# A spectral mixing layer and two feed-forward layers on one core: where the sum of real and imaginary part is made

## The chip, the cores and the metric

The kernel runs on one core of one Trainium2 chip. The metric is the device time of one execution in microseconds (us): 1951.52 as the median of three runs, which lie between 1948.21 and 1952.62.

The engines of a core work side by side, each through its own list of instructions in a fixed order, and wait for each other by semaphores. TensorE (PE in the rows) multiplies matrices and writes to PSUM, the small memory for its results; it loads the weights of a product in instructions of their own (PEld). VectorE (DVE) and ScalarE (ACT) read PSUM and the main on-chip memory, SBUF. GpSimd (POOL) and SyncE (SP) here only start transfers.

## The reference

Three layers follow each other, on 4 batches of 3072 rows with 256 columns. The first mixes along the rows by a real Fourier transform, a complex product with a bias, a soft threshold, and the transform back:

```
X = rfft(x, axis=1)
Yr = Xr @ w_r - Xi @ w_i + b_r
Yi = Xr @ w_i + Xi @ w_r + b_i
Y  = sign(Y) * max(|Y| - 0.01, 0)        # real and imaginary part apart
y  = irfft(Y)
```

The second shifts by one row, mixes with two vectors, and computes `sigmoid(xr @ w_r) * (relu(xk @ w_k)**2 @ w_v)` (hidden width 1024). The third computes `g = h * clip(h + 3, 0, 6) / 6` with `h = x @ w_in`, and then `g @ w_out` (hidden width 2048). Everything is float32.

## The kernel before

**The transform.** The 3072 rows are 96 by 32. Stage `s1` multiplies by a 96-point table over all rows of a batch; its results go to DRAM and come back in another order. Function `mid(b)` then does the middle of the transform for one batch in 12 steps `j`. Each step has four parts. `s2(j)` multiplies the data (as weights) by a table `t` (as the moving side): four products, one for each half of the frequencies `g` and of the 256 columns `dt`. In batches 1 to 3 the table has 192 columns, three groups of 64: real part, imaginary part, and their sum. The sum is a third set of table columns, so TensorE computes it. `mix(j)` makes the complex product from three real ones (sum times w_r, imaginary part times -(w_r + w_i), real part times w_i - w_r), adds the bias and applies the threshold. `split_y(j)` and `ia(j)` begin the transform back; `ib` ends it after another trip through DRAM.

**Precision.** A float32 product of `s2` is carried out as two passes on TensorE. The products after it are float32r, in one pass, and get their precision from splitting each operand into a high part and a rest: `split` rounds with a ScalarE copy (line 167) and subtracts with VectorE (line 168). So the result of `s2`, a PSUM tile of 128 x 768 numbers, becomes the tiles `Xh` and `Xl`. In `mix` each pair of operands takes three products (function `three`, line 176).

**Order.** The engines' order is that in which the code is written. The batches' middle stage is a generator, `stream(later)`, of which `feed()` takes one step at a time between the units of the second layer: `u_r` (tile `pr`), `u_k` (tile `pk`; the ReLU of line 719, the square of lines 723 and 727, the rest of line 728) and `u_v` (tile `acc`). A round of the middle stage is thus, on TensorE, a `pk` or `pr`, an `ia`, an `s2` (tile `s` in the rows), an `acc` and a `mix`. On VectorE a round has the square and its rest (727, 728), the threshold of the mix before (453), the rest of `s2` (`Xl`, 168), that of `split_y` (`yl`, 168), and the two sums after the mix (`yf`, 448 and 449); now and then also steps of `prep`, which makes the input of the next tile of the second layer (682, 690). On ScalarE it has the first half of the threshold (`ym`, 451), parts of `prep` (677, 688), the square's high part (`gh`, 723), the ReLU (719), the copy of `ia` (488), `Xh` (167) and `yh` (167).

**PSUM.** The results of `pk`, `pr`, `s2`, `mix`, `ia`, `s1` and `ib` share three buffers that are taken in turn (`ptile`). A product into a buffer waits until the third one before it has been read. In the middle stage `s2` thus often takes the buffer of a `mix`, and waits for line 449, which reads it last. A `pk` or an `ia` takes that of an `s2`, and waits for `Xl`.

The lines that the change touches are in `_tables` (the order of the table's columns), `load_t` (which columns are loaded), `s2` and `part` of `mix`:

Of the kernel before, what the change touches and what calls it, by code (L numbers as in the profile page):

```python
# [9 lines left out]
F32 = mybir.dt.float32  # L10
# [3 lines left out]
AF = mybir.ActivationFunctionType  # L14
# [7 lines left out]
NP = NG // 2  # L22
# [4 lines left out]
BEHIND = 3  # L27
# [18 lines left out]
def _pair(a):  # L46
    hi = _round12(a)
    return hi, (a - hi.astype(np.float64)).astype(np.float32)


def _tables():

    th = 2 * np.pi / S
    n1 = np.arange(N1)
    n2 = np.arange(N2)
    f1 = np.zeros((N1, N1))
    f1[:, 0] = 1.0
    f1[:, 1] = (-1.0) ** n1
    for u in range(1, 48):
        f1[:, 2 * u] = np.cos(2 * np.pi * u * n1 / N1)  # L60
        f1[:, 2 * u + 1] = -np.sin(2 * np.pi * u * n1 / N1)
    fwd = np.zeros((NP, 2, 2, 2, N2, 4, N2))
    inv = np.zeros((NP, 2, 2, 2, N2, 2, 2, N2))
    for g in range(NG):
        for uu in range(2):
            u = 2 * g + uu
            m = np.zeros((2, N2, 2, N2))
            w = np.zeros((2, N2, 2, N2))
            if u:
                k = u + N1 * np.arange(N2)  # L70
                s = np.where(k <= S // 2, 1.0, -1.0)
                c, z = np.cos(th * np.outer(n2, k)), np.sin(th * np.outer(n2, k))
                m[0, :, 0], m[1, :, 0] = c, z
                m[0, :, 1], m[1, :, 1] = -z * s, c * s
                w[0, :, 0], w[1, :, 0] = c.T * 2 / S, (-z * s).T * 2 / S
                w[0, :, 1], w[1, :, 1] = z.T * 2 / S, (c * s).T * 2 / S
            else:
                for j in range(N2):
                    src = 0 if j < 16 else 1
                    f = N1 * j if j < 16 else N1 // 2 + N1 * (j - 16)  # L80
                    c, z = np.cos(th * f * n2), np.sin(th * f * n2)
                    if j == 0:
                        alt = (-1.0) ** n2
                        m[0, :, 0, 0], m[0, :, 1, 0] = 1.0, alt
                        w[0, 0, 0], w[1, 0, 0] = 1.0 / S, alt / S
                    else:
                        m[src, :, 0, j], m[src, :, 1, j] = c, -z
                        w[0, j, src], w[1, j, src] = c * 2 / S, -z * 2 / S
            m = np.concatenate([m, m.sum(2, keepdims=True), 0 * m[:, :, :1]], 2)
            if u == 0:  # L90
                m[0, :, 2, 0], m[0, :, 3, 0] = 1.0, alt - 1.0
                m[:, :, 0:2, 0] = 0.0
            fwd[g // 2, uu, g % 2] = m
            inv[g // 2, uu, :, g % 2, :, g % 2] = w
    ext = np.zeros((128, N2), np.float32)
    ext[0:64] = fwd[0, 0, 0, :, :, 3].reshape(64, N2)
    fwd = fwd[:, :, :, :, :, 0:3].transpose(0, 1, 3, 4, 2, 5, 6)
    wide = np.zeros((NP, 2, 2, N2, 2, 3, 2, N2))
    for uu in range(2):
        wide[:, uu, :, :, :, :, uu] = fwd[:, uu]  # L100
    tab = np.zeros((NP + BEHIND, 128, 2, 448), np.float32)
    tab[:NP, :, :, 0:192] = wide.reshape(NP, 128, 2, 192)
    by_part = inv.reshape(NP, 2, 128, 128).transpose(0, 2, 1, 3)
    tab[BEHIND :, :, :, 192:448] = np.concatenate(_pair(by_part), 3)
    tab0 = np.zeros((NP + BEHIND, 128, 2, 224), np.float32)
    tab0[:NP, :, :, 0:96] = fwd.reshape(NP, 128, 2, 96)
    by_half = inv.reshape(NP, 2, 2, 64, 128).transpose(0, 1, 3, 2, 4)
    place = np.arange(128).reshape(4, 8, 4).transpose(1, 0, 2).ravel()
    tab0[BEHIND :, :, :, 96:224] = by_half.reshape(NP, 128, 2, 128)[..., place]
    rows = np.arange(N1).reshape(NP, 2, 2, 2).transpose(0, 2, 1, 3).reshape(-1)  # L110
    small = np.concatenate([f1, f1.T[rows]], 1).astype(np.float32)
    return [np.ascontiguousarray(a) for a in (tab, tab0, ext, small)]
# [3 lines left out]
def fourier_mix_ffn_kernel(  # L116
# [20 lines left out]
    nc = tc.nc  # L137
# [19 lines left out]
    def pad(pool, n):  # L157

        pads.append(n)
        pool.tile([128, n // 4], F32, name=f"pad{len(pads)}")  # L160

    def ptile(name):
        return ps.tile([128, 1024], F32, tag="h", name=name)

    def split(src, h, l):

        nc.scalar.activation(h, src, AF.Copy)
        nc.vector.tensor_sub(l, src, h.bitcast(F32))
# [86 lines left out]
    with tc.manual_schedule(engines=order):  # L255
        ff = ctx.enter_context(ExitStack())
        fp = ff.enter_context(tc.tile_pool(name="fp", bufs=1, side="right"))
# [40 lines left out]
        def take(n):  # L298

            u = head["use"]  # L300
            load_chunks(u + n)
            r = [live.pop(u + i) for i in range(n)]
            head["use"] = u + n
            return r
# [52 lines left out]
        def load_t(b, j):  # L357

            if j >= NP + BEHIND:
                b, j = b + 1, j - NP - BEHIND  # L360
            if b < B:
                if pad_t:
                    pad(fp, pad_t.pop())
                t = fp.tile([128, 2, 448], F32R if b else F32, tag="t", bufs=3, name="tt")
                n, w = (192, 448) if b else (96, 224)
                c = slice(0 if j < NP else n, n if j < BEHIND else w)
                nc.gpsimd.dma_start(out=t[:, :, c], in_=(tab if b else tab0)[j, :, :, c])
                tt[b, j] = t

        def mid(b):  # L370
# [9 lines left out]
            def s2(j):  # L380
                (a,) = take(1)
                t = tt[b, j].bitcast(F32) if b else tt[b, j]
                p = ptile("s2")
                if pad_x:
                    pad(fp, pad_x.pop())
                xh = fp.tile([128, 896], F32R, tag="Xh", bufs=2, name="Xh")
                xl = fp.tile([128, 896], F32R, tag="Xl", bufs=2, name="Xl")
                mm = lambda o, lhs, rhs: nc.tensor.matmul(o, lhs, rhs, start=True, stop=True)  # L388
                for g in range(2):
                    for dt in range(2):  # L390
                        d = slice(128 * dt, 128 * dt + 128)
                        if b:
                            o = p[:, 512 * dt : 512 * dt + 384].rearrange("p (k h g f) -> p k h g f", k=3, h=2, g=2)
                            mm(o[:, :, :, g], a[:, g, d], t[:, g, 0:192])
                        else:
                            for h in range(2):
                                k = slice(64 * h, 64 * h + 64)
                                c = 512 * h + 192 * dt
                                o = p[:, c : c + 192].rearrange("p (k g f) -> p k g f", k=3, g=2)
                                mm(o[:, :, g], a[k, g, d], t[k, g, 0:96])  # L400
                        if not (j or g):
                            c = 384 + (512 if b else 32) * dt
                            k = slice(0, 128 if b else 64)
                            mm(p[:, c : c + 32], a[k, g, d], tex[k])
                if b:
                    v = p.rearrange("p (dt f) -> p dt f", dt=2)
                    w = lambda x: x[:, 0:768].rearrange("p (dt f) -> p dt f", dt=2)
                    split(v[:, :, 0:384], w(xh), w(xl))
                    e = v[:, :, 384:416]
                else:  # L410
                    v = p.rearrange("p (h f) -> p h f", h=2)[:, :, 0:384].rearrange("p h (c f) -> p h c f", f=64)
                    w = lambda x: x[:, 0:768].rearrange("p (c h f) -> p h c f", c=6, h=2)
                    split(v, w(xh), w(xl))
                    e = p[:, 384:448].rearrange("p (dt f) -> p dt f", dt=2)
                if not j:
                    w = lambda x: x[:, 768:832].rearrange("p (dt f) -> p dt f", dt=2)
                    split(e, w(xh), w(xl))
                xx[j] = (xh, xl)

            def mix(j):  # L420
                xh, xl = xx.pop(j)
                p = ptile("mix")
                k1 = p[:, 512:768]

                def part(k):
                    cs = [slice(384 * dt + 128 * k, 384 * dt + 128 * k + 128) for dt in range(2)]
                    if k == 3:
                        cs = [slice(768 + 32 * dt, 800 + 32 * dt) for dt in range(2)]
                    return [((xh[:, c], xl[:, c]), dt) for dt, c in enumerate(cs)]
# [807 lines left out]
```

## Time and profile before

| | us |
|---|---|
| median of three runs | 1951.52 |
| the profiled execution | 1950.81 |
| its span, first to last instruction | 1948.6 |
| PE busy | 1916.4 (98%) |
| DVE busy | 1419.5 (73%) |
| ACT busy | 1237.6 (64%) |
| mean granted clock of TensorE | 0.993 |

The middle stages of batches 1 to 3 lie between about 145 and 252, 336 and 452, and 527 and 642 us of the span. The rest of the time up to about 990 us belongs to the other stages of the transform and the second layer, and the time from there to the third layer. The profile's busy time of PE counts pipelined products with modelled ends; a gap between two of them is time in which TensorE waited.

### The profile page before, as it was taken

Reading aid. Unit: us, or ns where it says so; the run is one execution under the profiler, and the core shown is the slowest. Engines: PE = TensorE matmul, PEld = TensorE weight load, DVE = VectorE, ACT = ScalarE, POOL = GpSimd, SP = SyncE. Lnnn points to the kernel's source line nnn. Section 1 sums busy time; section 2 is a strip of 40 time slices with the busy share of each in tenths; the row PEclk is TensorE's granted clock in tenths of the full one; section 3 lists DMA queues with packets and bytes.
Section 4 is the critical chain, followed back from the end, with each engine's and each line's share of the span. In section 5 each row is a group of like instructions: output and inputs, shape, how many; then the busy total and the mean of one; then the engine's idle time right before and its main releaser. Section 6 shows DMA issues by size and latency. Waiting matters only on the chain.

```text
span 1948.6 us, 32994 instructions
## 1 busy us (share of the span) xinstructions
PE 1916.4 (98%) x13512; PEld 1756.6 (90%) x13512; DVE 1419.5 (73%) x1770; ACT 1237.6 (64%) x1770; POOL 136.5 (7%) x245
## 2 busy tenths in 40 slices
PE   8989999999999999999999999999999999999998
PEld 5778878887888788888899999999999999999998
DVE  3867655675566657787688777887778887788876
ACT  3665554556445457777567767676677766677765
POOL 2402320222022100000000000000000000000000
PEclk8989999999999999999999999999999999999999
DMA  8784567456634442221101001010010100011000
GB/s 274 220 265 139 155 179 237 118 145 198 223 103 122 135 152 77 84 91 67 44 23 34 23 23 33 23 33 23 23 28 28 33 23 23 24 33 34 23 12 23
DMA packets 106593, 172.80 MB, mean 89 GB/s; under 512 B 13827, under 2 KB 63795, under 8 KB 106443
## 3 DMA queue, kind: packets, MB, share of 16 engines
q1 hardware_dynamic: 88714, 132.87, 21.6%
q0 software_dynamic: 17296, 37.53, 7.3%
q8 instruction: 106, 1.74, 0.4%
q14 instruction: 45, 0.36, 0.1%
q10 hardware_dynamic: 432, 0.30, 0.1%
HBM read 97.71 MB, written 63.31 MB: 83 GB/s over the span
## 4 chain that ended last, share of the span: by engine, by line
PE 92%; DVE 4%; DMA 1%; ACT 1%; issue 1%; SPq 0%; POOL 0%; ACTq 0%; DVEq 0%; POOLq 0%
PE oacc L988 26%; PE rq L988 16%; PE acc L176 13%; PE pk L176 13%; PE cc L988 6%; PE mix L176 4%; PE pr L176 3%; PE s L388 3%; PE ib L575 3%; PE s L323 2%; PE ia L176 1%; PE pi L176 1%; DVE g L920 0%; DMA a<-sc_b 0%; ACT g L916 0%
## 5 line engine op out<-in xcount | busy, mean ns | idle before, releaser
L988 PE MATMUL oacc<-wo_hi,gl 128*128 128x256 f32 x1536 | 425.2, 277 | 1.2 <-DVE gl L929 1.2
L988 PE MATMUL oacc<-wo_hi,gh 128*128 128x256 f32 x1536 | 425.3, 277 | 0.0
L988 PE MATMUL oacc<-wo_lo,gh 128*128 128x256 f32 x1536 | 424.7, 276 | 0.0
L988 PEld LDWEIGHTS oacc<-wo_hi,gl 128*128 128x128 f32 x1536 | 288.7, 188 | 1.8 <-DVE gl L929 1.6
L988 PEld LDWEIGHTS oacc<-wo_hi,gh 128*128 128x128 f32 x1536 | 288.4, 188 | 0.2
L988 PEld LDWEIGHTS oacc<-wo_lo,gh 128*128 128x128 f32 x1536 | 288.5, 188 | 0.0
L920 DVE SCALAR_TENSOR_TENSOR g<-g,c 128x1024 f32<-128x1024 f32 x184 | 225.5, 1225 | 50.2 <-ACT g L916 47.5
L929 DVE TENSOR_TENSOR gl<-g,gh 128x1024 fp32r<-128x1024 f32 x184 | 225.2, 1224 | 41.2 <-ACT gh L926 41.2
L916 ACT ACTIVATE g<-c,half 128x1024 f32<-128x1024 f32 x184 | 212.2, 1153 | 4.9 <-DVE c L911 4.9
L988 PE MATMUL rq<-th,sw 128*128 128x256 f32 x1104 | 206.1, 276 | 0.0
L906 ACT ACTIVATE s<-rq 128x256 f32<-128x256 f32 x184 | 70.5, 383 | 209.6 <-PE rq L988 209.5
L926 ACT ACTIVATE gh<-g 128x1024 fp32r<-128x1024 f32 x184 | 193.8, 1053 | 1.7 <-DVE g L920 1.6
L910 DVE TENSOR_TENSOR c<-rq,s 128x512 f32<-128x512 f32 x184 | 126.6, 688 | 89.1 <-ACT s L906 89.0
L988 PEld LDWEIGHTS rq<-th,sw 128*128 128x128 f32 x1104 | 166.3, 188 | 0.2 <-ACT s L895 0.2
L176 PE MATMUL pk<-kh,wk_hi 128*128 128x512 f32 x384 | 156.3, 407 | 0.4 <-DVE yf L449 0.4
L176 PE MATMUL acc<-gh,wv_hi 128*128 128x512 f32 x384 | 155.0, 404 | 0.0
L988 PE MATMUL rq<-tl,sw 128*128 128x256 f32 x552 | 152.5, 276 | 0.7 <-DVE tl L864 0.7
L176 PE MATMUL acc<-gl,wv_hi 128*128 128x512 f32 x384 | 150.7, 392 | 0.5 <-DVE gl L728 0.5
L176 PE MATMUL acc<-gh,wv_lo 128*128 128x512 f32 x384 | 150.3, 391 | 0.0
L176 PE MATMUL pk<-kl,wk_hi 128*128 128x512 f32 x384 | 150.2, 391 | 0.0
L176 PE MATMUL pk<-kh,wk_lo 128*128 128x512 f32 x384 | 149.6, 390 | 0.0
L727 DVE TENSOR_TENSOR g<-g 128x1024 f32<-128x1024 f32 x76 | 92.9, 1222 | 77.5 <-ACT gh L723 77.0
(174 smaller groups left out, 4449.6 us busy)
## 6 DMA issues: line engine op xcount, KB each, us to landing
yt<-sc_y SPq DMA_DIRECT2D x23, 608.0 KB, 3.9
sc_a<-s1sb SPq DMA_DIRECT2D x32, 384.0 KB, 6.5
a<-sc_a SPq DMA_DIRECT2D x48, 256.0 KB, 3.3
sc_b<-iasb SPq DMA_DIRECT2D x48, 256.0 KB, 4.1
sc_y<-ysb SPq DMA_DIRECT2D x32, 384.0 KB, 2.6
sc_x<-r SPq DMA_DIRECT2D x24, 512.0 KB, 2.8
xa<-sc_x SPq DMA_DIRECT2D x24, 512.0 KB, 3.8
tt<-in_tab_dram POOLq DMA_DIRECT2D x27, 448.0 KB, 3.8
```

The source lines that it names most:

```text
L176: nc.tensor.matmul(o, a, c, start=first and i == 0, stop=last and i == n - 1, **kw)
L323: nc.tensor.matmul(p[:N1, 512 * i : 512 * i + 512], f1, a, start=True, stop=True)
L388: mm = lambda o, lhs, rhs: nc.tensor.matmul(o, lhs, rhs, start=True, stop=True)
L575: nc.tensor.matmul(p[:, q, et, i], lhs, fi, start=True, stop=True)
L727: nc.vector.tensor_mul(g, g, g)
L906: nc.scalar.activation(s[:, 3], q, AF.Copy)
L910: nc.vector.tensor_add(c[:, 1::2], two(rq), s[:, 0:2])
L916: nc.scalar.activation(g, c, AF.Relu, bias=half, scale=1.0 / 6.0)
L920: nc.vector.scalar_tensor_tensor(g, g, 1.0, tmp["c"], op0=ALU.min, op1=ALU.mult)
L926: nc.scalar.activation(h, tmp["g"], AF.Copy)
L929: nc.vector.tensor_sub(hg[i, j][1], tmp["g"], hg[i, j][0].bitcast(F32))
L988: return lambda: nc.tensor.matmul(o, lhs, rhs, start=start, stop=stop, skip_group_check=True)
```

## The change

For the steps `j` from 1 on in batches 1 to 3, `s2` multiplies only by the 128 table columns of the real and imaginary part, and the sum is made from the two results. The table's three groups are put in the order sum, real, imaginary; the load leaves the first group out. ScalarE copies the imaginary part (128 x 2 x 128) from PSUM to a new SBUF tile `im`; VectorE adds it to the real part and writes the sum into the free third of the PSUM tile; ScalarE makes the high part of real and imaginary in one instruction and that of the sum in a second; VectorE makes the rest in one, as before. Step 0 of each batch, with its special columns, and batch 0 stay as they were. `mix` finds its operands under the new order of the groups.

```diff
-        wide[:, uu, :, :, :, :, uu] = fwd[:, uu]
+        wide[:, uu, :, :, :, :, uu] = fwd[:, uu][..., (2, 0, 1), :]
...
-                c = slice(0 if j < NP else n, n if j < BEHIND else w)
+                c = slice((64 if b and j else 0) if j < NP else n, n if j < BEHIND else w)
...
-                            mm(o[:, :, :, g], a[:, g, d], t[:, g, 0:192])
+                            k = 1 if j else 0
+                            mm(o[:, k:, :, g], a[:, g, d], t[:, g, 64 * k : 192])
...
-                    split(v[:, :, 0:384], w(xh), w(xl))
+                    if j:
+                        s = fp.tile([128, 2, 128], F32, tag="im", bufs=1, name="im")
+                        nc.scalar.activation(s, v[:, :, 256:384], AF.Copy)
+                        nc.vector.tensor_add(v[:, :, 0:128], v[:, :, 128:256], s)
+                        nc.scalar.activation(w(xh)[:, :, 128:384], v[:, :, 128:384], AF.Copy)
+                        nc.scalar.activation(w(xh)[:, :, 0:128], v[:, :, 0:128], AF.Copy)
+                        nc.vector.tensor_sub(w(xl), v[:, :, 0:384], w(xh).bitcast(F32))
+                    else:
+                        split(v[:, :, 0:384], w(xh), w(xl))
...
                 def part(k):
+                    if b and k < 3:
+                        k = (k + 1) % 3
```

The engines' order follows the code. On ScalarE, around step 4 of batch 3 (the tile `s` is the PSUM tile of `s2`, `iasb` the copy of `ia`; the semaphores that a row waits for stand in brackets), these are the rows of before:

```order
L719 ACTIVATE g<-pk 128x1024 [waits PE_49]
L488 ACTIVATE iasb<-ia 128x512 [waits PE_49]
L167 ACTIVATE Xh<-s_4982 128x768 [waits PE_49]
L167 ACTIVATE yh<-yz 128x512 [waits DMASW2_49,DMASW3_49,DMASW1_49,DMASW0_49]
L688 ACTIVATE kh<-xf 128x1024 [waits DVE_49]
L723 ACTIVATE gh<-g 128x1024 [waits Activation_49]
```

and these the rows of the changed kernel at the same place, with its own line numbers:

```order
L730 ACTIVATE g<-pk 128x1024 [waits PE_49]
L499 ACTIVATE iasb<-ia 128x512 [waits PE_49]
L411 ACTIVATE im<-s_5082 128x256 [waits PE_49]
L413 ACTIVATE Xh<-s_5082 128x2x256 [waits DVE_49]
L414 ACTIVATE Xh<-s_5082 128x2x128
L167 ACTIVATE yh<-yz 128x512 [waits DMASW2_49,DMASW3_49,DMASW1_49,DMASW0_49]
L699 ACTIVATE kh<-xf 128x1024
L734 ACTIVATE gh<-g 128x1024 [waits Activation_49]
```

One instruction has become three, and the second of them waits for VectorE; `yh`, `kh` and `gh` stand behind it.

On VectorE at the same place, before:

```order
L727 TENSOR_TENSOR g<-g 128x1024 [waits Activation_49]
L728 TENSOR_TENSOR gl<-g,gh 128x1024 [waits DVE_49]
L682 SCALAR_TENSOR_TENSOR xf<-yt,mus,xf 128x512 x2
L453 SCALAR_TENSOR_TENSOR yf<-ym,yf 128x512
L168 TENSOR_TENSOR Xl<-s_4982,Xh 128x768 [waits Activation_49]
L168 TENSOR_TENSOR yl<-yz,yh 128x512 [waits DMASW2_49,DMASW1_49,DMASW3_49,DMASW0_49,Activation_49]
L727 TENSOR_TENSOR g<-g 128x1024 [waits Activation_49]
```

and after:

```order
L738 TENSOR_TENSOR g<-g 128x1024 [waits Activation_49]
L739 TENSOR_TENSOR gl<-g,gh 128x1024 [waits DVE_49]
L693 SCALAR_TENSOR_TENSOR xf<-yt,mus,xf 128x512 x2
L464 SCALAR_TENSOR_TENSOR yf<-ym,yf 128x512
L412 TENSOR_TENSOR s_5082<-s_5082,im 128x2x128 [waits Activation_49]
L415 TENSOR_TENSOR Xl<-s_5082,Xh 128x768 [waits Activation_49]
L168 TENSOR_TENSOR yl<-yz,yh 128x512 [waits DMASW2_49,DMASW1_49,DMASW3_49,DMASW0_49,Activation_49]
L738 TENSOR_TENSOR g<-g 128x1024 [waits Activation_49]
```

The sum has been put in between the threshold of the mix before and `Xl`; nothing else has moved.

## Rows read from the trace of the kernel before

**Rows 1.** Busy time by stretch: us, each engine with (instructions), clock, DMA share, GB/s.

```profile
120.00:226.00 106.00, 106.00 (x606) 93.38 (x604) 77.97 (x97) 60.19 (x81) 19.14 (x36) 1.00 0.55 168
```

**Rows 2.** Timeline of TensorE: start, us, engine, line, operation, tiles, shape, merged count, [idle before].

```profile
559.64 1.46 PE L388 MATMUL s<-tt,a 128*128 128x192 f32 x8
...
96.56 2.00 PE L575 MATMUL ib<-fi,rows 96*128 96x96 f32 x16 [0.21 <-DMA stw<-in_moe_w_v_dram]
```

**Rows 3.** Timeline of TensorE, the three passes of s2 before which it waited.

```profile
227.51 1.54 PE L388 MATMUL s<-tt,a 128*128 128x192 f32 x8 [1.36 <-issue]
...
398.56 1.54 PE L388 MATMUL s<-tt,a 128*128 128x192 f32 x8 [1.38 <-issue]
...
571.48 1.62 PE L388 MATMUL s<-tt,a 128*128 128x192 f32 x8 [2.06 <-issue]
```

**Rows 4.** Timeline of VectorE ahead of the third of these waits, batch 3.

```profile
547.50 0.69 DVE L448 TENSOR_TENSOR yf<-mix,bias 128x512 f32<-128x512 f32 x1 [1.70 <-PE mix L176]
...
554.66 0.95 DVE L168 TENSOR_TENSOR Xl<-s,Xh 128x768 fp32r<-128x768 f32 x1
...
557.98 0.69 DVE L449 TENSOR_TENSOR yf<-yf,mix 128x512 f32<-128x512 f32 x1
561.69 1.22 DVE L727 TENSOR_TENSOR g<-g 128x1024 f32<-128x1024 f32 x1 [3.02 <-ACT gh L723]
...
566.02 0.95 DVE L168 TENSOR_TENSOR Xl<-s,Xh 128x768 fp32r<-128x768 f32 x1
...
567.58 1.23 DVE L727 TENSOR_TENSOR g<-g 128x1024 f32<-128x1024 f32 x1
...
570.70 0.69 DVE L449 TENSOR_TENSOR yf<-yf,mix 128x512 f32<-128x512 f32 x1
```

**Rows 5.** Timeline of ScalarE in the same stretch.

```profile
551.53 0.81 ACT L167 ACTIVATE Xh<-s 128x768 fp32r<-128x768 f32 x1
...
558.76 0.72 ACT L451 ACTIVATE ym<-yf,lam 128x512 f32<-128x512 f32 x1 [3.44 <-DVE yf L449]
...
562.47 0.58 ACT L488 ACTIVATE iasb<-ia 128x512 f32<-128x512 f32 x1
562.94 0.81 ACT L167 ACTIVATE Xh<-s 128x768 fp32r<-128x768 f32 x1
563.63 0.63 ACT L167 ACTIVATE yh<-yz 128x512 fp32r<-128x512 f32 x1
565.53 1.06 ACT L688 ACTIVATE kh<-xf 128x1024 fp32r<-128x1024 f32 x1 [1.27 <-DVE xf L682]
566.50 1.05 ACT L723 ACTIVATE gh<-g 128x1024 fp32r<-128x1024 f32 x1
```

**Rows 6.** Groups by line and shape: busy us, mean ns, idle before and its releaser.

```profile
L906 ACT ACTIVATE s<-rq 128x256 f32<-128x256 f32 x184 | 70.5, 383 | 209.6 <-PE rq L988 209.5
L168 DVE TENSOR_TENSOR Xl<-s,Xh 128x64 fp32r<-128x64 f32 x4 | 0.9, 224 | 1.2 <-ACT Xh L167 1.2
L910 DVE TENSOR_TENSOR c<-rq,s 128x512 f32<-128x512 f32 x184 | 126.6, 688 | 89.1 <-ACT s L906 89.0
```

**Rows 7.** Timeline of VectorE in batch 1, three rounds ahead of the wait at 227.

```profile
184.17 0.95 DVE L168 TENSOR_TENSOR Xl<-s,Xh 128x768 fp32r<-128x768 f32 x1
...
192.98 0.95 DVE L168 TENSOR_TENSOR Xl<-s,Xh 128x768 fp32r<-128x768 f32 x1
...
199.49 0.96 DVE L168 TENSOR_TENSOR Xl<-s,Xh 128x768 fp32r<-128x768 f32 x1 [2.10 <-ACT Xh L167]
...
203.53 0.69 DVE L448 TENSOR_TENSOR yf<-mix,bias 128x512 f32<-128x512 f32 x1 [1.16 <-PE mix L176]
```

**Rows 8.** Timeline of VectorE in batch 2, the same place ahead of the wait at 398.

```profile
374.56 0.69 DVE L448 TENSOR_TENSOR yf<-mix,bias 128x512 f32<-128x512 f32 x1 [1.16 <-PE mix L176]
```

**Rows 9.** Busy time around the first wait and after the third, columns as in rows 1.

```profile
200.00:250.00 50.00, 48.64 (x284) 43.49 (x283) 34.96 (x44) 27.02 (x37) 13.85 (x26) 1.00 0.49 142
...
572.00:577.00 5.00, 5.00 (x19) 4.14 (x18) 3.82 (x6) 3.70 (x6) 2.65 (x5) 0.66 0.46 114
```

## The prediction

> **What bounds the kernel now.** I read the busy time by stretch first, then TensorE's waits, then the timelines of the two engines that it waits for. TensorE is busy in all of the 106 us from 120 to 226, in which most of the middle stage of batch 1 lies, while VectorE has 78 and ScalarE 60 [rows 1]. So a shorter product there is time saved, as long as the other two keep pace. But once in each of the three batches they don't: TensorE waits 1.36, 1.38 and 2.06 us before a step of `s2` [rows 3]. The trace names no releaser. The third of these `s2` starts at 571.48, and line 449 on VectorE, the last reader of the PSUM buffer that this `s2` takes, runs from 570.70 for 0.69, so to 571.39 [rows 3, 4]. It is VectorE's delay, not a transfer. How it comes about: ScalarE's `ym` (451) can only start when line 449 is done (557.98 + 0.69, and 558.76), behind `ym` stands `gh` (723), and VectorE's square (727) waits for `gh`: it had idled 3.02 us [rows 4, 5]. Mix, 449, `ym`, `gh`, square, `Xl`, the next 449 form a ring over two engines that takes as long as a round of TensorE. The change puts work into it.
>
> **What it removes.** In 33 steps (11 in each of 3 batches) there are 4 products of 2 passes, 264 passes in all, with 128 columns instead of 192. Eight passes take 1.46 us [rows 2], the last one of about 0.33 (its two passes' length; a pass is longer than the distance to the next), so they start every (1.46 - 0.33)/7 = 0.162. That is in proportion to columns 0.108 for 128. A pass of 96 columns, the `ib` products, starts every (2.00 - 0.28)/15 = 0.115 [rows 2], more than in proportion (0.081), so there is a floor. I take 0.113 for 128 columns, between 0.108 and 0.115. Saved: 264 x 0.049 = 12.9 us of TensorE's time (12.4 to 14.3). The table loads shrink by 64 of 384 or 448 columns; TensorE waits for none of them in these stretches, so nothing for that, nor for the new order of the groups.
>
> **What it adds.** In each of the 33 steps, the one `Xh` of ScalarE (0.81) is replaced by a copy of 256 numbers (0.38, as the copy of that shape in PSUM [rows 6]), one of 512 (0.58, as `iasb` [rows 5]) and one of 256 (0.38). VectorE gets an addition of 256 numbers out of PSUM into PSUM. No row has one. A subtraction of 64 takes 0.22, one of 768 takes 0.95 [rows 4, 6], so 256 on that line is 0.22 + 192 x 0.00104 = 0.42; the bounds are 0.22 and the 0.69 of 512 [rows 6]. I take 0.42.
>
> The second ScalarE instruction waits for the addition, as its row in the order shows. All of ScalarE's later work stands behind it. There are two cases. Where VectorE is early (it idled 2.10 before `Xl` at 199.49 [rows 7]), the chain from the end of `s2` is 0.04 + 0.38 + 0.04 + 0.42 + 0.04 + 0.58 + 0.38 - 0.10 + 0.04 = 1.82 instead of 0.87, so `Xl` comes 1.0 later (0.04 is a handover, 0.10 the overlap of two instructions of ScalarE in sequence). Where VectorE is late, so that `Xl` starts without idle, ScalarE's copy has long been made, and `Xl` comes 0.42 + 0.04 + 0.58 + 0.38 - 0.10 + 0.04 = 1.4 later; and ScalarE, which was done with `Xh` long before, now stands still until VectorE gets to the addition.
>
> **The third wait worked through.** At 547.50 VectorE had idled 1.70, so nothing is carried in [rows 4]. The round's `Xl` (554.66, no idle) moves by 1.4, to 556.0, and with it everything up to line 449, which ends at 560.1 instead of 558.7. `ym`, `gh` and the square at 561.69 move by 1.4. VectorE would have started the next `Xl` at 566.02 and now starts the addition there, plus 1.4: 567.4, done at 567.84. Only now can ScalarE go on: the two copies end at 568.74, `yh` (0.63) at 569.3, `kh` (1.06) at 570.25, `gh` (1.05) at 571.2. Before, `gh` ended at 566.50 + 1.05 = 567.55 [rows 5], and the square on VectorE followed at 567.58 [rows 4]. It now starts at 571.24, 3.7 later, and line 449 and the waiting `s2` move by 3.7. TensorE had come early to this wait, and stands still all the longer: what it saved in the batch before this point is gone.
>
> **The first two waits.** They end the same two rounds, so 3.7 each. Something is carried in here: two rounds with a late VectorE (184.17 and 192.98; batch 2 has the same sequence) bring 1.4 each and a round with an early one 1.0, and VectorE's idle before line 448, 1.16 in either batch, takes back that much [rows 7, 8]: 1.4 + 1.4 + 1.0 - 1.16 = 2.6. The rounds in between don't give it back, since the ring is closed; bounds 0 and 2.6, and I take 2.6.
>
> **TensorE's clock.** After the wait of 2.06 the granted clock fell to its lower level (1.2 GHz of 2.4) for part of what follows: 0.66 of full speed in the mean of 572 to 577, so 5 x 0.34 = 1.7 us lost. After the wait of 1.36 it did not fall: 1.00 from 200 to 250 [rows 9]. If the first two waits grow past 2.06, each brings such a fall: 2 x 1.7 = 3.4.
>
> **The sum.** 3 x 3.7 + 2 x 2.6 = 16.3 later. Kept is only what is saved from the wait on: 3 steps in batch 1, 5 in batch 2, 7 in batch 3, 15 x 8 x 0.049 = 5.9. With the clock 16.3 - 5.9 + 3.4 = +13.8. The profiled execution took 1950.8 (its span is 1948.6), so 1964.6. The median is 0.7 above it, and I say 1965. From what is unknown: the addition between 0.22 and 0.69 moves ten late rounds by -2.0 to +2.7; without carrying, 5.2 less; without the clock, 3.4 less. The forecast's own range is 1956 to 1976.
>
> A rule of the Trainium skill bears on the wait of the second ScalarE instruction, which I count fully. Its page "PSUM — Partial Sum Buffer", section "PSUM bank collisions raise a hardware error", says that two engines must not access one PSUM bank in the same partitions at once, at whatever addresses, so that this copy and the addition, which lie in the same banks, have to come one after the other. If they could overlap, a late round would cost 0.42 + 0.04 + 0.38 + 0.04 = 0.9 instead of 1.4. No run here shows them at once.
>
> **Rivals.**
> *The slack holds it all* (chance 0.15). VectorE has 28 us of idle in the 106 of rows 1, ScalarE 46, and most `s2` follow without a wait. Then all 12.9 arrive: 1938. Against it: idle in such a ring is mostly the other engine's turn, and the three waits show that there is none left at their places.
> *The delays cancel the saving* (0.13). If ScalarE's standing still did not reach `gh`, each wait would grow by 1.4 alone, without a carry and without a fall of the clock: 3 x 1.4 - 5.9 = -1.7, so 1949, no change. For it speaks that `kh` had waited 1.27 for VectorE before [rows 5]; against it that `gh` is needed at once.
> *The ring becomes the bound of every round* (0.08). If each of the 33 steps pays 1.4, and no idle takes any back: 33 x 1.4 = 46, so 1997.
> *The passes don't get shorter* (0.04). If loading the weights kept them at 0.162, nothing is kept: 13.8 + 5.9 = 19.7 more, 1970. The 0.115 of `ib` speaks against it.
> The forecast itself has the rest, 0.60.
>
> **How the numbers follow.** A measurement of this kernel tells about 0.2% from no change, 3.9 us. Faster than 1947.6: the first rival, 0.15. Within: the second, 0.13. Slower than 1955.4: the forecast, the third and the fourth, 0.72. The range has to leave out no more than 0.2: 1942 leaves out most of the first rival (0.12), 1984 leaves out the third (0.08).
>
> **What would show it.** The passes of `s2` with 128 columns should start 0.11 apart. ScalarE's copy of the imaginary part should be followed by idle up to the addition in about ten of 33 steps, 3 us long at the worst. The waits of TensorE before `s2` should grow from 4.8 us in sum to over 15, with a fall of the clock in every batch, while the stages from 650 us on stay as long as they are. I am wrong if these waits stay under 5 us (then it is the first rival).

## The result and the profile after

The changed kernel takes 1971.95 us (median of four runs, 1968.82 to 1972.87) against 1951.32 for the kernel before in the same comparison: 1.0106 of its time, 95% interval 1.0093 to 1.0119. It is slower by about 21 us; 1965 was predicted. The spans of the profiled executions are 1971.1 and 1948.6 us, a difference of 22.5.

TensorE first. These are the steps of `s2` in the timeline of TensorE after the change that answer to those of before ([rows 2, 3]); the first is the first step with a shorter product, the last one of those that had no wait:

```profile
150.97 1.06 PE L388 MATMUL s<-tt,a 128*128 128x128 f32 x8
...
234.82 2.05 PE L388 MATMUL s<-tt,a 128*128 128x128 f32 x8 [3.96 <-issue]
...
413.36 2.04 PE L388 MATMUL s<-tt,a 128*128 128x128 f32 x8 [3.96 <-issue]
...
593.01 2.04 PE L388 MATMUL s<-tt,a 128*128 128x128 f32 x8 [3.97 <-issue]
604.89 1.05 PE L388 MATMUL s<-tt,a 128*128 128x128 f32 x8
```

Eight passes now take 1.05 instead of 1.46. With the last pass at 0.27 to 0.28 they start every (1.05 - 0.275)/7 = 0.111 us: the product became shorter by 264 x 0.051 = 13.5 us in sum. But the three waits are 3.96 to 3.97 instead of 1.36, 1.38 and 2.06, and the eight passes behind them take 2.04, twice as long: the granted clock is at its lower level there (0.50 of full speed in every us from 234 to 240). TensorE's other waits in the table of waits (engine, line, what it waited for: us in sum, times, longest):

```profile
PE s L388 <- issue: 11.9, 3, 4.0
...
PE pk L176 <- DVE Xl L415: 5.4, 3, 2.2
PE pk L176 <- DVE yf L460: 3.2, 4, 1.4
PE ia L176 <- DVE yl L168: 3.1, 2, 2.1
PE ia L176 <- DVE Xl L415: 2.7, 4, 1.0
PE ia L176 <- DVE yf L460: 2.3, 1, 2.3
```

So TensorE does not only wait at the three places: `pk` and `ia` now wait for VectorE's instructions of the mixing too. The table of busy time (columns as in [rows 1]) gives the sum, with the long stretch after and a line of before to compare it with:

```profile
120.00:700.00 580.00, 547.31 (x3006) 460.62 (x3005) 365.98 (x460) 308.16 (x457) 107.02 (x189) 0.98 0.53 153
```

```profile
120.00:700.00 580.00, 569.83 (x3133) 487.65 (x3132) 367.38 (x443) 306.17 (x404) 103.09 (x189) 0.99 0.55 164
```

TensorE stands still for 580 - 547.3 = 32.7 us of the 580 after, and for 10.2 before. The 15 us from the end of each of the three waits on, after the change:

```profile
234.82:249.82 15.00, 14.99 (x75) 13.14 (x76) 8.76 (x12) 8.57 (x15) 5.59 (x10) 0.82 0.39 105
413.36:428.36 15.00, 15.00 (x77) 13.18 (x78) 9.25 (x12) 9.05 (x16) 5.58 (x10) 0.85 0.42 116
593.01:608.01 15.00, 15.00 (x74) 13.13 (x75) 8.66 (x12) 8.47 (x15) 5.58 (x10) 0.81 0.36 92
```

TensorE works through these 15 us, and a granted clock of 0.82, 0.85 and 0.81 is 2.7, 2.2 and 2.8 us lost. The clock falls already while TensorE still stands (0.72 in the us from 233 to 234); that part costs nothing and isn't counted. Before, the same view gives 1.00 behind the first two waits and this behind the third, 15 x 0.11 = 1.65 us:

```profile
571.48:586.48 15.00, 15.00 (x75) 13.18 (x76) 9.07 (x11) 8.74 (x13) 5.29 (x10) 0.89 0.42 113
```

The third layer has not changed: from its first product (`pi`, at 949.6 us before and 972.1 after) to the end of the span it takes 999.0 us in both.

Now the ring ahead of the third wait. The timeline of VectorE after the change, answering to [rows 4]:

```profile
565.43 0.69 DVE L459 TENSOR_TENSOR yf<-mix,bias 128x512 f32<-128x512 f32 x1 [0.76 <-PE mix L176]
...
572.60 0.42 DVE L412 TENSOR_TENSOR s<-s,im 128x256 f32<-128x256 f32 x1
573.96 0.96 DVE L415 TENSOR_TENSOR Xl<-s,Xh 128x768 fp32r<-128x768 f32 x1 [0.94 <-ACT Xh L414]
...
581.00 1.22 DVE L738 TENSOR_TENSOR g<-g 128x1024 f32<-128x1024 f32 x1 [3.03 <-ACT gh L734]
...
585.33 0.42 DVE L412 TENSOR_TENSOR s<-s,im 128x256 f32<-128x256 f32 x1
586.69 0.96 DVE L415 TENSOR_TENSOR Xl<-s,Xh 128x768 fp32r<-128x768 f32 x1 [0.94 <-ACT Xh L414]
...
589.10 1.22 DVE L738 TENSOR_TENSOR g<-g 128x1024 f32<-128x1024 f32 x1 [0.85 <-ACT gh L734]
...
592.22 0.69 DVE L460 TENSOR_TENSOR yf<-yf,mix 128x512 f32<-128x512 f32 x1
```

And ScalarE's timeline beside it, answering to [rows 5]:

```profile
582.25 0.38 ACT L411 ACTIVATE im<-s 128x256 f32<-128x256 f32 x1
585.79 0.60 ACT L413 ACTIVATE Xh<-s 128x512 fp32r<-128x512 f32 x1 [3.16 <-DVE s L412]
586.28 0.38 ACT L414 ACTIVATE Xh<-s 128x256 fp32r<-128x256 f32 x1
586.54 0.63 ACT L167 ACTIVATE yh<-yz 128x512 fp32r<-128x512 f32 x1
587.06 1.06 ACT L699 ACTIVATE kh<-xf 128x1024 fp32r<-128x1024 f32 x1
588.01 1.06 ACT L734 ACTIVATE gh<-g 128x1024 fp32r<-128x1024 f32 x1
```

ScalarE has copied the imaginary part at 582.63 and stands still for 3.16 us until VectorE reaches the addition at 585.33. `gh` stands behind that, and so VectorE itself waits 0.85 for `gh` at the square. Two late rounds pass like this, and line 460 ends at 592.91, when the `s2` at 593.01 can start. In all 33 steps ScalarE stands still 49.7 us before its second copy, 1.9 to 3.2 us in 14 of them and 0.5 in each of the others, and VectorE 31.0 us before `Xl`.

### The profile page after: what moved, and what is told of

Its sections match the earlier page's. It is cut to its first block, busy times and chain, and to the rows that moved or that the text cites. A ratio compares the mean times of both kernels' runs of the same rounds, so it can differ in the third digit from the quotient of the medians.

```text
span 1971.1 us, 33117 instructions
## 1 busy us (share of the span) xinstructions
PE 1916.8 (97%) x13512; PEld 1749.4 (89%) x13512; DVE 1432.9 (73%) x1803; ACT 1249.6 (63%) x1836; POOL 140.3 (7%) x245
## 3 DMA queue, kind: packets, MB, share of 16 engines
q1 hardware_dynamic: 88714, 132.87, 21.5%
q8 instruction: 106, 1.74, 0.4%
## 4 chain that ended last, share of the span: by engine, by line
PE 82%; DVE 9%; ACT 4%; issue 3%; DMA 1%; POOL 0%; ACTq 0%; DVEq 0%; SPq 0%
PE oacc L999 25%; PE rq L999 15%; PE acc L176 10%; PE pk L176 10%; PE cc L999 6%; PE pr L176 3%; PE ib L586 3%; PE s L323 3%; PE mix L176 2%; PE s L388 2%; DVE g L738 1%; DVE gl L739 1%; PE pi L176 1%; ACT gh L734 1%; DVE yf L460 1%
```

## The experiments

"Before" is timed anew on the chip of each comparison; its medians there were 1949.2 to 1950.6. Three questions: what the shorter product is worth by itself, which part of the added work costs, and where in the ring the cost lies.

**The shorter product alone (e1).** The sum is not made: its third of the columns is filled from the real part again, so the rounding and the subtraction keep their 768 columns and no instruction is added.

```diff
-                        nc.scalar.activation(s, v[:, :, 256:384], AF.Copy)
-                        nc.vector.tensor_add(v[:, :, 0:128], v[:, :, 128:256], s)
...
+                        thrice = v[:, :, 128:256].rearrange("p dt (a f) -> p dt a f", a=1).to_broadcast([128, 2, 3, 128])
+                        by3 = lambda x: w(x).rearrange("p dt (a f) -> p dt a f", a=3)
+                        split(thrice, by3(xh), by3(xl))
```

> The 128-column passes alone: no sum is made; the one rounding copy and the one subtraction keep their 768 columns, filled with the real part three times (so the mixing's operands are not the right ones; its work is the same). Theory (the ring of VectorE and ScalarE, lengthened by the sum, is what costs): without the sum the 264 shorter passes, 13.5 us by the changed kernel's 0.111 us a pass, are nearly all kept; lost are those of the two rounds ahead of each of the three waits, about 2.5 us, so about 1940 us. Rival (a shorter product only brings TensorE earlier to waits that stay where they are): 1948 to 1952.

Measured: 1936.02 (runs from 1934.69 to 1943.83), 0.994 of before (0.9919 to 0.9961): 13.2 us faster by the medians, about 12 by the ratio. Most of the 13.5 us arrives. The shorter product works, and what the change loses it loses by the added instructions.

**The new instructions with the long product (e2).** The table is loaded and multiplied in full as before, the sum made as in the change.

```diff
-                c = slice((64 if b and j else 0) if j < NP else n, n if j < BEHIND else w)
+                c = slice(0 if j < NP else n, n if j < BEHIND else w)
...
-                            k = 1 if j else 0
+                            k = 0
```

> The changed kernel with the whole table of 192 columns loaded and multiplied again in every step: only what the sum costs, without what the shorter passes save. Theory (savings ahead of a batch's long wait are lost, only those of the 15 steps from the waits on are kept): 15 x 8 x 0.051 = 6 us more than the changed kernel, 1976 to 1980 us. Rival (saving and cost simply add up): 13.5 us more, 1985 us.

Measured: 1980.47, 1.0161 (1.0144 to 1.0178), just above the first theory's range and below the rival's 1985. The added work by itself costs 30 us, and the shorter product earns about 9 of its 13.5 beside it (8.5 by the medians of the two comparisons, 11 by their ratios). The rest is lost in standing still: of the 580 us from 120 to 700 TensorE stands 26.7 here and 32.7 in the change. The three waits before `s2` are 11.9 us in sum in both, so the difference lies at its other waits.

**A wait and almost no work (e4).** The kernel before, with an addition of zero to 2 columns of the PSUM tile on VectorE in the 33 steps. It takes 0.16 us, and ScalarE's one copy has to wait for it.

```diff
+                    if j:
+                        nc.vector.tensor_add(v[:, :, 0:1], v[:, :, 0:1], zero)
                     split(v[:, :, 0:384], w(xh), w(xl))
```

> The kernel before, with only the wait: VectorE adds zero to two columns of the PSUM tile of s2 (about 0.07 to 0.15 us of work), at the place where the changed kernel has the sum, and ScalarE's rounding copy has to wait for it. Theory (ScalarE stands still until a late VectorE gets there, and the square's high part behind it comes late): the rest of s2 comes 1.0 later in late rounds, the high part up to 3 us, so each of the three waits grows by about 3, with falls of the clock: 1964 to 1974 us. Rival (VectorE's work is the cause): 0.1 us in 33 steps, under 1954 us.

Measured: 1969.61, 1.0104 (1.0089 to 1.012): 33 x 0.16 = 5.3 us of VectorE's time cost 20 us, as much as the whole change. ScalarE's timeline in this kernel shows the same standstill before the copy:

```profile
582.73 0.81 ACT L167 ACTIVATE Xh<-s 128x768 fp32r<-128x768 f32 x1 [3.17 <-DVE s L409]
...
584.90 1.05 ACT L725 ACTIVATE gh<-g 128x1024 fp32r<-128x1024 f32 x1
```

and its timeline of TensorE the same wait:

```profile
589.89 2.58 PE L388 MATMUL s<-tt,a 128*128 128x192 f32 x7 [3.97 <-issue]
```

**The work without the wait (e3).** The kernel before, with an addition on VectorE as long as that of the change, of tiles for whose result nobody waits.

```diff
+                    if j:
+                        s = fp.tile([128, 2, 128], F32, tag="im", bufs=1, name="im")
+                        nc.vector.tensor_add(s, bias[:, 0].rearrange("p (a n) -> p a n", a=2), bias[:, 1].rearrange("p (a n) -> p a n", a=2))
```

> The kernel before, with only VectorE's extra work: an addition of 2 x 128 columns in SBUF, about 0.42 us, stands ahead of the rest of s2 in each of the 33 steps; nobody waits for it. Theory (what costs is above all ScalarE's standing still and the longer chain over both engines): 0.42 in two late rounds ahead of each wait, 2.5 us, and up to 3 to 7 us more if the longer waits let TensorE's clock fall: 1954 to 1960 us. Rival (VectorE has too much work, and its 0.42 in each step is the cause): most of what the sum cost, over 1968 us.

Measured: 1954.24 (eight runs, from 1951.24 to 1956.72), 1.0024 (1.0013 to 1.0035), 5 us slower. The three waits before `s2` are 6.5 us in sum, against 4.8 before and 11.9 in e4. 33 x 0.42 = 13.9 us of VectorE's time cost 5, a wait with 5.3 us of it costs 20. What is dear in these two kernels is that ScalarE waits, with `gh` queued behind.

**The rounding moved to the second half of the round (e5).** Copy and addition stay; the rounding (again one instruction) and `Xl` come behind `gh` and the square on their engines.

```diff
+                        def rounded():
+                            nc.scalar.activation(w(xh), v[:, :, 0:384], AF.Copy)
+                            nc.vector.tensor_sub(w(xl), v[:, :, 0:384], w(xh).bitcast(F32))
+                        late.append(rounded)
...
+                while late:
+                    late.pop()()
                 if j:
                     rest = mix(j - 1)
```

> The changed kernel with the rounding copy (one instruction of 768 columns again) and the rest of s2 moved into the second half of the round, ahead of the mixing: ScalarE no longer stands at the addition, since by then it has long been made; the work is that of the changed kernel less one instruction of ScalarE. Theory: the wait goes and VectorE's 0.42 stays, so nearly all of the 13.5 us is kept: 1938 to 1946 us. Rival (VectorE's work is the cause): it stays, over 1964 us.

Measured: 1952.92, 1.0014 (1.0004 to 1.0023). 19 us of the change's loss go with the standstill, but the expected gain over before (1938 to 1946) did not come. A wait that I had not foreseen took its place. In TensorE's timeline:

```profile
575.76 0.77 PE L176 MATMUL ia<-yh,tt 128*128 128x256 f32 x2 [3.31 <-DVE Xl L417]
```

`ia` takes the PSUM buffer of an earlier `s2`, and its last reader `Xl` now stands behind the square and the subtraction, as VectorE's timeline shows:

```profile
572.26 1.23 DVE L744 TENSOR_TENSOR g<-g 128x1024 f32<-128x1024 f32 x1 [0.54 <-ACT gh L740]
573.52 1.22 DVE L745 TENSOR_TENSOR gl<-g,gh 128x1024 fp32r<-128x1024 f32 x1
574.67 0.95 DVE L417 TENSOR_TENSOR Xl<-s,Xh 128x768 fp32r<-128x768 f32 x1
```

**VectorE rounds the sum (e7).** ScalarE copies the imaginary part and rounds the two others without waiting; VectorE adds and rounds the sum.

```diff
-                        nc.vector.tensor_add(v[:, :, 0:128], v[:, :, 128:256], s)
                         nc.scalar.activation(w(xh)[:, :, 128:384], v[:, :, 128:384], AF.Copy)
-                        nc.scalar.activation(w(xh)[:, :, 0:128], v[:, :, 0:128], AF.Copy)
+                        nc.vector.tensor_add(v[:, :, 0:128], v[:, :, 128:256], s)
+                        nc.vector.tensor_copy(w(xh)[:, :, 0:128], v[:, :, 0:128])
```

> The changed kernel, but VectorE also makes the high part of the sum, and ScalarE's copy of real and imaginary part stands ahead of the addition, so that ScalarE waits for VectorE nowhere; VectorE gets a second instruction of 256 columns (about 0.42 us) in each of the 33 steps. Theory (the wait is the cause): twice the vector work of the experiment with 0.42 alone (which cost 0.24%, 4.7 us) less the 13.5 us of the passes: 1942 to 1950 us. Rival (VectorE's work is the cause in this kernel, where the passes are short): over 1965 us.

Measured: 1960.06, 1.0052 (1.0037 to 1.0067), between the two theories. Taking ScalarE's wait away gives 12 us back, although VectorE gets a second instruction of 0.42. But the waits before `s2` are still 3.03: the first two are 1.7 longer than before, which is 0.85 of VectorE's work in each of two late rounds. The kernel is 9.5 us slower than before and loses the 13.5 of the shorter product as well, 23 in all, where 0.42 alone with the long product cost 5 (e3). So the standstill is not the whole cost: with the short product VectorE's own row of instructions is dear too. How much of the change's loss is the one and how much the other, no run shows.

**The sum on GpSimd (e6).** From the rounded and remaining parts in SBUF; VectorE and ScalarE split only the two other thirds.

```diff
+                        h, l = w(xh), w(xl)
+                        split(v[:, :, 128:384], h[:, :, 128:384], l[:, :, 128:384])
...
+                        hf, lf = h.bitcast(F32), l.bitcast(F32)
+                        nc.gpsimd.tensor_add(s, hf[:, :, 128:256], hf[:, :, 256:384])
+                        nc.gpsimd.tensor_add(s, s, lf[:, :, 128:256])
+                        nc.gpsimd.tensor_add(s, s, lf[:, :, 256:384])
+                        nc.gpsimd.tensor_copy(h[:, :, 0:128], s)
+                        nc.gpsimd.tensor_sub(l[:, :, 0:128], s, hf[:, :, 0:128])
```

> The sum on GpSimd, out of the split parts in SBUF: three additions, a rounding copy and a subtraction of 256 columns in each of the 33 steps; ScalarE's copy and VectorE's subtraction shrink from 768 to 512 columns (0.2 and 0.26 us less). Theory: the ring of VectorE and ScalarE gets shorter than before, so the 13.5 us are kept and the three waits shrink: 1932 to 1940 us, as long as GpSimd's five instructions take under about 4 us a step. Rival (TensorE is held by the middle stage's chain in any engine, or GpSimd is too slow and holds back the transfers it starts): 1950 us or more.

Measured: 1963.21, 1.0064 (1.0049 to 1.0079). A miss, and the expectation's own condition failed: from the start of the first to the end of the last, GpSimd's five instructions take 3.7 to 6.2 us a step, 4.8 in the mean and over 4 in 26 of the 33. One reason is that GpSimd and VectorE hold each other up. GpSimd's timeline, then VectorE's of the same time:

```profile
579.29 0.73 POOL L414 TENSOR_TENSOR sm<-Xh 128x256 f32<-128x256 f32 x1
580.10 1.60 POOL L415 TENSOR_TENSOR sm<-sm,Xl 128x256 f32<-128x256 f32 x1
```

```profile
578.11 1.23 DVE L741 TENSOR_TENSOR g<-g 128x1024 f32<-128x1024 f32 x1 [0.27 <-ACT gh L737]
579.37 1.75 DVE L742 TENSOR_TENSOR gl<-g,gh 128x1024 fp32r<-128x1024 f32 x1
```

VectorE's subtraction of two SBUF operands takes 1.75 instead of 1.23, while GpSimd's first addition runs; the second addition takes 1.60 instead of 0.75, while the subtraction runs. `mix` waits for GpSimd's results eight times, 7.9 us in sum, and the three waits before `s2` are 8.4 us in sum, so they did not shrink. How much of the loss comes from the holding up, no run shows.

**The edge in the ring that the square adds (e8 to e11).** VectorE's square writes over `g`, which ScalarE's `gh` reads, so the square waits for `gh` ([rows 4], 3.02 us). The tag of `g` has two buffers. One edit lets the square have the second one; only the subtraction behind it still waits for `gh`. It was made in four kernels: the changed one (e8), before (e9), the one in which VectorE rounds the sum (e10) and the one with the late rounding (e11).

```diff
+                q = kb.tile([128, 1024], F32, tag="g", bufs=2, name="q")
                 nc.scalar.activation(h, g, AF.Square)
...
-                    nc.vector.tensor_mul(g, g, g)
-                nc.vector.tensor_sub(l, g, h.bitcast(F32))
+                    nc.vector.tensor_mul(q, g, g)
+                nc.vector.tensor_sub(l, q, h.bitcast(F32))
```

> The changed kernel, with one edge taken out of the ring: VectorE's square goes into a tile of its own (the second buffer of the same tag), so it no longer waits for ScalarE's gh, which reads the same g; only the subtraction behind it still does. Theory (the two engines form a ring in which each added microsecond ahead of line 460 comes back as a wait of TensorE): in either of the two rounds ahead of a wait the square, 1.22 us, moves into VectorE's idle time ahead of it (3.03 and 0.85 us in batch 3), so line 460 comes 2.1 to 2.4 earlier; the three waits before s2 shrink from 3.97 to about 1.7, the falls of the clock get shorter: 1972 less 7 less 5, 1956 to 1963. Rival (ScalarE alone is what is late, by standing still until the addition): its standstill is set by the addition, which stands behind work that waits for gh as before, so 1968 to 1974.

> The kernel before, with the same edit as in the run above and nothing of the change. Theory: the ring has 2.1 to 2.4 us more slack, so the waits of 1.36, 1.38 and 2.06 before s2 are gone, and the fall of the clock with them: 1951 less 4.8 less 1.7, 1943 to 1947. Rival: 1949 to 1953, as before.

> The kernel in which VectorE also rounds the sum, so that ScalarE never waits for VectorE between its copies, with the same edit. Theory: its three waits before s2 of 3.03 shrink by 2.1 to 2.4, to under 1, and most of the shorter passes is kept: 1940 to 1948, so it beats both kernels. Rival (VectorE is simply full in these rounds, so that an edge less brings nothing): 1956 to 1961.

> The kernel in which the rounding and Xl stand in the second half of the round, with the same edit. Theory: Xl stands behind the square and what follows; these come 1.2 to 2.4 earlier, so the waits of ia for the PSUM buffer (3.3 us) shrink to 1 to 2: 1943 to 1949. Rival: 1950 to 1955, as without the edit.

| kernel | without the edit | with it | of before (interval) | TensorE still, 120 to 700 us |
|---|---|---|---|---|
| before (e9) | 1949.56 | 1938.08 | 0.9942 (0.9928 to 0.9957) | 10.2, then 1.7 |
| changed (e8) | 1971.95 | 1938.73 | 0.9948 (0.9931 to 0.9965) | 32.7, then 11.3 |
| VectorE rounds (e10) | 1960.06 | 1933.18 | 0.9918 (0.9904 to 0.9933) | 22.4, then 8.8 |
| late rounding (e11) | 1952.92 | 1929.22 | 0.9898 (0.9884 to 0.9913) | 18.5, then 4.4 |

All four gain more than I expected: 11.5 us on before, 33 on the change, 27 and 24 on the others (the last three from two comparisons each; by their ratios to before 31, 26 and 23). The timeline of VectorE in the changed kernel with this edit, in the two late rounds ahead of the third wait:

```profile
557.00 1.22 DVE L739 TENSOR_TENSOR q<-g 128x1024 f32<-128x1024 f32 x1
560.05 1.22 DVE L740 TENSOR_TENSOR gl<-q,gh 128x1024 fp32r<-128x1024 f32 x1 [1.83 <-ACT gh L735]
...
565.96 1.22 DVE L739 TENSOR_TENSOR q<-g 128x1024 f32<-128x1024 f32 x1
...
569.14 0.69 DVE L460 TENSOR_TENSOR yf<-yf,mix 128x512 f32<-128x512 f32 x1
```

The idle time of 3.03 has become 1.83 and a square; that of 0.85 has gone, and ScalarE's standstill ahead of `Xh` is 1.74 instead of 3.16. TensorE still waits 2.86 or 2.87 us before the same three `s2`, against about 1.7 expected, for now nothing else holds it up on the way there; but `pk` and `ia` wait hardly at all, and the clock falls behind one of the three waits instead of all. The gain is larger than the waits that I had reckoned with, since I had counted the three `s2` alone. On before the gain of 11.5 can be accounted for: TensorE stands still 8.5 us less, and two falls of the clock are gone, 1.7 us each. One is that behind the third `s2`; the other, at 665 us behind a wait of 2.10 of an `ia` (clock 0.89 from 663 to 678), I had not counted.

The change's own time without the edit is from the first comparison, those of e10 and e11 from theirs. With the slack the change can be judged by itself. As it is made it is worth nothing: 1938.73 against 1938.08. With the rounding late it is worth 8.9 us (1929.22 against 1938.08, with runs from 1929.19 to 1929.96 and 1937.39 to 1938.45), of the 13.5 that TensorE saves. The last is the fastest kernel here, 1.0% under before.

## Why the prediction was right, and where not

The mechanism, its place and its sign were as predicted, but the sum was 13.8, and the spans differ by 22.5 (the medians by 20.6). The delay can be read along the way, at rows that both traces have. VectorE's line 448 (459 after) at the starts of the walks ([rows 4, 7, 8]) has these two rows after, beside the one at 565.43 shown above:

```profile
207.25 0.68 DVE L459 TENSOR_TENSOR yf<-mix,bias 128x512 f32<-128x512 f32 x1
...
385.78 0.68 DVE L459 TENSOR_TENSOR yf<-mix,bias 128x512 f32<-128x512 f32 x1
```

and the first step with a shorter product stood here in TensorE's timeline of before:

```profile
149.79 1.47 PE L388 MATMUL s<-tt,a 128*128 128x192 f32 x8
```

| up to | before | after | later by | this stretch | predicted |
|---|---|---|---|---|---|
| first shorter product | 149.79 | 150.97 | 1.2 | 1.2 | 0 |
| line 448, batch 1 | 203.53 | 207.25 | 3.7 | 2.5 | 2.6 (carry) |
| first wait's `s2` | 227.51 | 234.82 | 7.3 | 3.6 | 3.7 |
| line 448, batch 2 | 374.56 | 385.78 | 11.2 | 3.9 | 2.6 - 1.2 + 1.7 = 3.1 |
| second wait's `s2` | 398.56 | 413.36 | 14.8 | 3.6 | 3.7 |
| line 448, batch 3 | 547.50 | 565.43 | 17.9 | 3.1 | -2.0 + 1.7 = -0.3 |
| third wait's `s2` | 571.48 | 593.01 | 21.5 | 3.6 | 3.7 |
| end of the span | 1948.6 | 1971.1 | 22.5 | 1.0 | -2.7 |

*The passes and the new instructions.* 0.111 us a pass where 0.113 was estimated, 13.5 us where 12.9. The addition takes 0.43 where 0.42 was taken, the copies 0.38, 0.60 and 0.38. Right. The 0.115 of the 96-column passes had an idle ahead in it; a row of `ib` without one (16 passes in 1.92 us, at 140.71 in the trace of before) gives (1.92 - 0.28)/15 = 0.109. So, as far as `ib` shows, 128 columns are at the floor already.

*The walk to the wait.* 3.6, three times, where 3.7 was worked out, with ScalarE's standstill of 3.16 and the handover by `gh`. Right. The idle of 1.16 ahead of line 448 is gone, as the carry of 2.6 had it (2.5). That most of these 3.6 come from ScalarE's wait and not from VectorE's 0.42 us is shown by e4 and e3: with the wait and 0.16 of work the three waits are 11.9 us in sum, as in the change, with 0.42 and no wait 6.5.

*The clock.* Too small. I took 1.7 us for a fall and counted two more of them. The waits of 3.96 brought 2.7, 2.2 and 2.8, and the third, which had 1.7 before, grew too: 7.7 - 1.7 = 6.0 instead of 3.4. I had taken the price of a fall from the one after a wait of 2.06, although I expected waits of over 3.7.

*"Kept is only what is saved from the wait on", 5.9.* This failed: of the 8.7 us between 13.8 and 22.5 the two stretches behind the second and the third wait have 3.4 and 3.7. It supposes that TensorE runs freely behind its waits. It does not: in batch 2 `ia` waits 2.27 for line 460, and `pk` twice about half a us, where before only one wait of 0.98 stood. TensorE's timeline after, then before:

```profile
444.97 0.50 PE L176 MATMUL pk<-kh,wk_hi 128*128 128x512 f32 x1 [0.49 <-ACT g L730]
...
455.04 0.47 PE L176 MATMUL pk<-kh,wk_hi 128*128 128x512 f32 x1 [0.60 <-DVE yf L460]
...
473.07 0.47 PE L176 MATMUL ia<-yh,tt 128*128 128x256 f32 x2 [2.27 <-DVE yf L460]
```

```profile
454.37 0.47 PE L176 MATMUL ia<-yh,tt 128*128 128x256 f32 x2 [0.98 <-DVE yf L449]
```

That is 3.4 - 1.0 = 2.4 us more of standing still; with 2.2 for the clock and -2.0 kept it makes 2.6, near the 3.1 of the table. Behind the third wait TensorE stands still 6.0 us, against 4.3 before; with 1.1 more for the clock that is 2.8 of the 3.7. (Between the first wait and batch 2 the term held: there the clock, 2.7 for 1.7, accounts for nearly all of the 3.9.) So the slack of the ring was gone in rounds that I had not walked: I had counted ten late rounds, and ScalarE's long standstills are 14. The other four are at 461 us in batch 2 and at 554, 641 and 652 in batch 3, three of them behind a wait. e1 shows the contrast: without the added instructions about 12 to 13 of the 13.5 us are kept.

*What the profile was to show.* The waits before `s2` were to exceed 15 us in sum and are 11.9: the delay arrives in full at these places, but TensorE stands still for part of it earlier, at `pk` and `ia`. ScalarE's longest standstill (3.2, where 3 was said), a clock that falls in every batch, and a third layer as before came as said.

*The rest.* 1.2 us lie ahead of the first changed step. They need not be the change's: in three more kernels whose code is that of before up to there this step starts at 149.27 (e9), 150.56 (e4) and 150.59 (e3), so such a difference comes from one execution to the next.

Of the rivals, "the slack holds it all" gave 1938; e1 comes to 1936 without the added instructions, and after the ring's edge was taken out e11 keeps 8.9 of the 13.5 with the additions, so it would need another kernel. "The passes don't get shorter" is excluded by the passes. "The delays cancel" has the waits at 1.4 more each, and they are 1.9 to 2.6 longer with 3.6 of delay. "The ring becomes the bound of every round" is half true: more rounds than three have a wait, but short ones.

On the rule of the Trainium skill, "PSUM — Partial Sum Buffer", section "PSUM bank collisions raise a hardware error": ScalarE's `Xh` starts 0.46 behind the addition's start in the rows above (585.79 and 585.33), so behind its end. That agrees, but the wait in the program forces it, and no run shows the two at once.

## What to carry to other kernels

When work moves from the busiest engine to two others, don't ask how busy those are, but which instruction is then queued behind a wait: 0.16 us with a wait in front of ScalarE's queue cost 20 us, 0.42 us without one cost 5. Look for an edge of the ring that only the reuse of a buffer makes, such as a result that is written over an operand which another engine still reads: taking it out was worth 11.5 us on the kernel before, and over 30 on the changed one. And where the bounding engine is made faster, walk the rounds behind its first wait as well as those ahead of it, since it will be early there too.

## What was not expected of the hardware

**A fall of the clock does not follow from the length of the wait ahead of it alone.** In e3 the waits before the three `s2` are 1.95, 1.95 and 2.64 us, in e10 1.97, 1.96 and 2.58. The table of busy time around them, of e3:

```profile
227.00:242.00 15.00, 13.11 (x67) 11.90 (x68) 10.14 (x14) 6.91 (x10) 4.46 (x9) 0.89 0.43 120
399.00:414.00 15.00, 13.05 (x69) 11.41 (x68) 11.40 (x15) 6.03 (x9) 3.97 (x9) 0.89 0.46 135
573.00:588.00 15.00, 12.36 (x62) 10.98 (x62) 12.00 (x16) 5.63 (x8) 4.89 (x10) 0.89 0.52 151
```

and of e10:

```profile
225.00:240.00 15.00, 14.56 (x90) 13.09 (x91) 11.24 (x16) 8.98 (x15) 5.60 (x10) 1.00 0.44 121
394.00:409.00 15.00, 15.00 (x95) 13.53 (x96) 10.69 (x15) 8.79 (x15) 5.60 (x10) 1.00 0.50 132
564.00:579.00 15.00, 15.00 (x95) 13.50 (x96) 10.70 (x15) 8.80 (x15) 5.60 (x10) 1.00 0.40 103
```

In e3 the clock fell to its level of 1.2 GHz for part of all three stretches, in e10 in none. Behind the wait TensorE is busy without a gap in both; what is missing of 15.0 us in e3's rows is the wait itself, most of which lies ahead of e10's stretches. After 2.86 it fell once in three times (e8), after 3.96 every time. What else decides stays open. These rows are of one execution of each kernel. The mean granted clock of e3's eight executions runs from 0.989, in the one shown, to 0.994, and their times from 1951.24 to 1956.72: the falls differ between executions of one kernel too.

**GpSimd and VectorE hold each other up in SBUF.** In e6 an addition of 256 numbers takes 0.74 us on GpSimd while VectorE stands still, as here,

```profile
190.41 0.74 POOL L416 TENSOR_TENSOR sm<-sm,Xl 128x256 f32<-128x256 f32 x1
```

and 1.60 behind the start of a VectorE subtraction with both operands in SBUF, in the rows of e6 above; that subtraction itself grows from 1.23 to 1.75 behind the start of a GpSimd addition (which takes 0.73). The Trainium skill, "SBUF — State Buffer", section "Who interferes with whom", says that a VectorE instruction with two operands in SBUF contends with a GpSimd instruction that reads SBUF. The trace agrees, with those numbers.
